# The last chunk ahead of a feed-forward: turned on TensorE, or by VectorE and DMAs through memory

## The chip, the cores and the metric

One Trainium2 chip, one of its cores. The metric is the device time of the whole program in microseconds (us), the median of several runs.

## The reference

Two transformer layers in float32 on 2048 tokens of width 448. Each layer is an attention with 16 query heads of width 28 that share one key and one value head, and a gated feed-forward of inner width 1792, both behind a layer normalization and added to the residual.

```python
x = A_x
x = x + _A_ref(_layernorm(x, axis=-1), A_wq, A_wk, A_wv, A_wo)
x = x + _B_ref(_layernorm(x, axis=-1), B_w_gate, B_w_up, B_w_down)
x = x + _A_ref(_layernorm(x, axis=-1), A_wq, A_wk, A_wv, A_wo)
x = x + _B_ref(_layernorm(x, axis=-1), B_w_gate, B_w_up, B_w_down)

def _B_ref(x, w_gate, w_up, w_down):
    g = _silu(x @ w_gate)
    u = x @ w_up
    return (g * u) @ w_down
```

## The kernel before

The 2048 tokens are cut into four chunks of 512 (`c` = 0 to 3), each of four tiles of 128 tokens. The residual `xres` stays in SBUF with tokens on the partitions. The matrix products want the normalized input turned, with the 448 features on the partitions, in three groups of 128 and one of 64, and split into a rounded high part and a rest (`xh`, `xl`), so that three products of rounded numbers stand for one of full ones. The last group of 64 features is kept twice, in the two halves of the partitions; `xd` holds a copy that this needs.

So between a normalization and a product a chunk has to be turned. The kernel has two ways for that:

- `flip` (L270) turns on TensorE: 16 transposes against an identity (L275) into PSUM banks, which ScalarE and VectorE then split into `xh` and `xl` (`flipped`, L278).
- `norm_steps(c, away=True)` (L213) turns without TensorE. For each of the four tiles VectorE normalizes into a side tile (`apply`, L234) and turns that in blocks of 32 x 32 into the tile `xn` (`turn`, L239). `send` (L248) writes `xn` to memory with four DMAs in an order that completes the turn, and `load` (L255, by way of `rows3`, L126) reads it back into another `xn` with two DMAs: one for the three full groups (L128), one that writes the last group to both halves (L129). `cut` (L265) splits from there.

Before the change chunks 0, 1 and 2 ahead of a feed-forward go the second way, spread over the attention's steps; the output projection of chunk 3 comes last, and chunk 3 goes the first way. Chunk 0 ahead of layer 1's attention goes the second way too (`hand_over`, L820). The side tile of the second way is `sg`, of which there is one, and which the feed-forward units use for their gate.

The feed-forward runs in units (`unit`, L853): one chunk of tokens by one slice of 128 of the inner width; two slices make a group, and a group goes over all four chunks. A unit with `xd` does on TensorE: first half of the gate and up products, then in the middle the first half of the down product of the unit before it (`pend`), then the second half of gate and up. Then ScalarE takes the gate's sigmoid product (L887), VectorE multiplies by up (L888), ScalarE rounds the product (L889), VectorE takes the rest (L892), and the second half of the earlier down product follows. Between the halves of a product ScalarE reads one column of each bank (`between`, L328), so that the second half does not begin before. After a chunk's last slice the sums are added to `xres` (L794 on VectorE, L797 and L798 on ScalarE and POOL).

The program's order on each engine and each DMA queue is the order in which this Python code issues instructions. Work that is to come later is put into lists: `soon` holds pairs of a number and a function, the number falls by one at the end of each unit, and the function is called there when it falls below zero; so 0 means the end of the next unit and 1 the end of the one after it. `mid[gi, c, n]` holds two functions for the middle of one unit, one ahead of the earlier unit's down product and one behind it.

`rest` (L918) begins the part of the feed-forward in which the change sits: the first units there are chunk 1 with slices 0 and 1, chunk 2 with slices 0 and 1, then chunk 3. Chunk 3 of the normalized input is prepared by these lines:

```python
            third, self.norms[3] = norm_steps(3)
            for f in third[:5]:
                f()
            self.soon.append([1, lambda: [f() for f in third[5:]]])
            self.mid[0, 2, 1] = [lambda ks=ks: self.turned(3, ks) for ks in ((0, 1), (2, 3))]
```

The statistics come at once, the normalization at the end of the unit of chunk 1 with slice 1, the transposes in the middle of the unit of chunk 2 with slice 1, two feature groups ahead of the down product and two behind it.

The DMAs named here are all issued from SyncE's queue, in order. The weight slices (`weights`, L157) are loaded there too, five DMAs each, into tiles of which there is one (`wr`, `wdr`); POOL splits them (L139, L140).

Of the kernel before, what the change touches and what calls it, by code (L numbers as in the profile page):

```python
# [8 lines left out]
F32 = mybir.dt.float32  # L9
# [6 lines left out]
P = 128  # L16
S = 2048
D = 448
# [34 lines left out]
def forward(  # L53
# [24 lines left out]
    pers = ctx.enter_context(tc.tile_pool(name="pers", bufs=1))  # L78
# [29 lines left out]
    def bank(cands, hold=False):  # L108

        for _ in cands:  # L110
            turn[cands] = (turn.get(cands, -1) + 1) % len(cands)
            b = cands[turn[cands]]
            if b not in live:
                if hold:
                    live.add(b)
                return b, banks[b]
        raise AssertionError("no bank")
# [5 lines left out]
    def dma(dst, src):  # L123
        nc.sync.dma_start(dst.bitcast(F32), src.bitcast(F32))

    def rows3(dst, src):  # L126
        n = src.shape[1]
        nc.sync.dma_start(dst[:, 0:3], src[0:384, :].rearrange("(k p) n -> p k n", p=P))  # L128
        nc.sync.dma_start(dst[:, 3], src[384:448, :][None].to_broadcast([2, 64, n]))  # L129

    def in_turn(cols):

        return cols.rearrange("p (n t) -> p t n", t=4)
# [71 lines left out]
    def xtile(pool, again=None):  # L205

        return (
            pool.tile([P, 4, 512], F32R, name="xh"),
            pool.tile([P, 3, 512], F32R, name="xl"),
            again,  # L210
        )

    def norm_steps(c, away=False):  # L213


        got = {}
        cs = slice(4 * c, 4 * c + 4)

        def stat(t):
            nc.vector.bn_stats(stats[:, 4 * c + t, :], xres[:, 4 * c + t, :])  # L220
            nc.vector.bn_aggr(mv[:, 4 * c + t, :], stats[:, 4 * c + t, :])

        def scale():
            rstd = pers.tile([P, 4], F32, name="rstd", bufs=2)
            nc.gpsimd.tensor_scalar(rstd, mv[:, cs, 1], 1.0, EPS, ALU.mult, ALU.add)
            nc.gpsimd.tensor_tensor(rstd, rstd, halfn, ALU.pow)
            got["r"] = rstd

        def apply(t):
            if t == 0:  # L230
                got["x"] = pers.tile([P, 4, 512], F32, name="xn")
            got["o"] = (pers.tile([P, 512], F32, name="sg") if away else got["x"][:, t, :])[:, 0:D]
            i, r = xres[:, 4 * c + t, :], got["r"][:, t : t + 1]
            nc.vector.tensor_scalar(got["o"], i, mv[:, 4 * c + t, 0:1], r, ALU.subtract, ALU.mult)  # L234
            if not away:
                nc.gpsimd.tensor_copy(got["x"][:, t, D:512], got["o"][:, 384:D])

        def turn(t):
            nc.vector.transpose(side()[:, :, :, t], got["o"].rearrange("p (k s) -> p k s", s=32))  # L239

        def side():
            return got["x"].rearrange("p t n -> p (t n)")[:, 0 : 4 * D].rearrange("p (k s t) -> p k s t", s=32, t=4)

        def send():
            turns.append(dram.tile([D, 512], F32, name=f"xt{len(turns)}"))
            got["xt"] = turns[-1]
            for a in range(4):
                nc.sync.dma_start(  # L248
                    got["xt"].rearrange("(k r) n -> r k n", r=32)[:, :, P * a : P * a + P],
                    side()[32 * a : 32 * a + 32].rearrange("p k s t -> p k (s t)"),  # L250
                )

        def load():
            got["raw"] = pers.tile([P, 4, 512], F32, name="xn")
            rows3(got["raw"], got["xt"])  # L255

        got["load"] = load
        fs = [lambda t=t: stat(t) for t in range(4)] + [scale]
        for t in range(4):
            fs += [lambda t=t: apply(t)] + [lambda t=t: turn(t)] * away  # L260
        return fs + [send] * away, got
# [3 lines left out]
    def cut(got, tiles, ks=range(4), copy=nc.scalar.copy):  # L265

        for k in ks:
            flipped(tiles, k, got["raw"][:, k, :], copy)

    def flip(got, tiles, ks=range(4)):  # L270

        for k in ks:
            pt = bank(wide[-1])[1]
            for t in range(4):
                nc.tensor.transpose(in_turn(pt)[:, t, :], got["x"][:, t, P * k : P * k + P], ident)  # L275
            flipped(tiles, k, pt, nc.scalar.copy)

    def flipped(tiles, k, pt, copy, steps=(0, 1)):  # L278

        xh, xl, xd = tiles  # L280
        twice = xd if k == 3 else None
        if 0 in steps and twice is None:
            copy(xh[:, k, :], pt)
        elif 0 in steps:
            copy(xh[0:64, k, :], pt[0:64, :])
            copy(xd[64:128, :], pt[64:128, :])
        if 1 in steps and k < 3:
            nc.vector.tensor_tensor(xl[:, k, :], pt, xh[:, k, :], ALU.subtract)
        elif 1 in steps:
            high = xh[64:128, k, :] if twice is None else xd[64:128, :]  # L290
            nc.vector.tensor_tensor(xh[64:128, k, :], pt[64:128, :], high, ALU.subtract)
# [40 lines left out]
    class Attention:  # L332
# [170 lines left out]
        def turned(self, c):  # L503
            if c in self.norms:
                flip(self.norms.pop(c), self.X[c])
# [245 lines left out]
    class FeedForward:  # L751
# [68 lines left out]
        def hand_over(self, c):  # L820

            a = self.nxt
            fs, got = norm_steps(c, c == 0)
            for f in fs[:5]:
                f()
            a.pool = self.stage
            a.X[c] = xtile(xpool if c < 2 else self.xbp)

            def ready():
                for f in fs[5:]:  # L830
                    f()
                a.norms[c] = got

            if c == 0:
                self.soon.append([1, lambda: [f() for f in fs[5:]]])
                self.soon.append([2, got["load"]])
                self.soon.append([4, lambda: cut(got, a.X[c])])
                self.soon.append([5, lambda: [a.project() for _ in range(3)]])
            elif c == 1:
                self.soon.append([2, ready])  # L840
            else:
                a.plan[4 * c - 4, 0] = [ready]

        def turned(self, c, ks=range(4)):
            flip(self.norms[c], self.X[c], ks)

        def flush(self):

# [68 lines left out]

        def rest(self, xb):  # L918
            self.stage = xb.enter_context(tc.tile_pool(name=f"stage{self.layer}", bufs=2, reuse_waits="tile"))
            self.xbp = xb.enter_context(tc.tile_pool(name=f"xb{self.layer + 1}", bufs=2, reuse_waits="tile"))  # L920
            xd = xb.enter_context(tc.tile_pool(name=f"xd{self.layer}", bufs=1, reuse_waits="tile"))
            self.xd = [xd.tile([P, 512], F32R, name=f"xd{c}") for c in range(NC)]
            for c in (0, 1):
                dma(self.xd[c][64:128, :], self.X[c][0][0:64, 3, :])
                self.X[c] = (*self.X[c][:2], self.xd[c])
            for c in (2, 3):
                self.X[c] = xtile(self.xbp, self.xd[c])
            cut(self.norms[2], self.X[2])
            third, self.norms[3] = norm_steps(3)
            for f in third[:5]:  # L930
                f()
            self.soon.append([1, lambda: [f() for f in third[5:]]])
            self.mid[0, 2, 1] = [lambda ks=ks: self.turned(3, ks) for ks in ((0, 1), (2, 3))]
            for gi, fs in enumerate(groups):
                if self.layer == 1 and fine is not None and gi in (2, 3):
                    self.verdict(gi == 3)
                    if gi == 3:
                        tc.mark_branch_hint_location("again", engines=(ET.Activation, ET.DVE, ET.Pool, ET.SP, ET.PE))
                for c in range(NC):
                    for n in range(len(fs)):  # L940
                        if gi or c:
                            self.unit(gi, c, n)
                if gi == len(groups) - 2 and self.nxt:
                    self.nxt.w = load_wqkv(xb.enter_context(tc.tile_pool(name="wqkv1", bufs=1, reuse_waits="tile")), None)[1]
            if self.nxt:
                self.nxt.project()
            self.flush()
# [7 lines left out]
    xb = ExitStack()  # L955
# [3 lines left out]
    fs, got = norm_steps(0)  # L959
# [28 lines left out]
    for c in range(1, NC):  # L988
        fs, got = norm_steps(c)
# [3 lines left out]
    for layer in range(2):  # L993
# [4 lines left out]
        xb = ExitStack()  # L998
# [30 lines left out]
```

## Time and profile before

| | us |
|---|---|
| median of 3 runs | 1986.77 |
| lowest and highest run | 1986.52, 1987.32 |
| span of the profiled execution, first to last instruction | 1984.8 |
| TensorE matmuls, busy | 1969.2 |
| ScalarE, busy | 1278.6 |
| VectorE, busy | 812.1 |
| POOL, busy | 528.7 |

The profiled execution's own time is its span; the timed runs lie some 2 us above it. In the rows of a timeline the columns are start and duration in us, engine, line, operation, the tiles it writes and reads, their shapes and how many such instructions are merged into the row; in brackets stands how long the engine was idle before it and what ended that. PE is TensorE, PEld its weight loads, DVE VectorE, ACT ScalarE, POOL GpSimd, and SPq the queue of SyncE, whose rows are the issues of DMAs and not their transfers. In the table by stretches of time, the columns are the stretch, its length, the busy time of PE, PEld, DVE, ACT and POOL with the number of instructions, the granted TensorE clock, the mean busy share of the 16 DMA engines, and GB/s.

### The profile page before, as it was taken

What the parts mean: (1) busy time and instruction counts of PE and PEld (TensorE: products, weight loads), DVE (VectorE), ACT (ScalarE), POOL (GpSimd) and SP (SyncE); (2) the same over time, 40 slices, a digit from 0 to 9 for tenths busy, and PEclk for the clock granted to TensorE, in tenths of its full rate; (3) what the DMA queues carried; (4) which work ended last, traced back from release to release, by engine and by line L of the source; (5) the groups of instructions that cost most, each with busy time, mean ns of one, the idle gap of its engine ahead of it and who ended that gap; (6) DMA issues with size and microseconds to landing.
All of it is one profiled execution on the core that took longest, in us unless ns stands there. A gap on an engine that the chain in (4) does not pass through costs nothing. (4 is left out here: it accounts for less than half of the span.)

```text
span 1984.8 us, 44687 instructions
## 1 busy us (share of the span) xinstructions
PE 1969.2 (99%) x18519; PEld 1322.9 (67%) x18519; DVE 812.1 (41%) x1410; ACT 1278.6 (64%) x2140; POOL 528.7 (27%) x571
## 2 busy tenths in 40 slices
PE   9999999999999999999999999999999999999998
PEld 7544545445458999999984444454454789988887
DVE  7444543544434222322554335445454432222222
ACT  4899797997953333333349998979979433333332
POOL 4212111132213233333341221111231232233320
PEclk9999999999999999999999999999999999999999
DMA  5101020121210011100131111102111101011102
GB/s 163 55 23 31 23 51 21 32 58 28 72 33 9 24 32 32 32 24 19 51 107 35 30 31 30 44 12 61 32 55 45 31 17 30 18 31 32 32 1 76
DMA packets 93382, 77.52 MB, mean 39 GB/s; under 512 B 23510, under 2 KB 76374, under 8 KB 93174
## 3 DMA queue, kind: packets, MB, share of 16 engines
q1 hardware_dynamic: 92886, 74.16, 13.5%
q8 instruction: 146, 2.39, 0.5%
q14 instruction: 62, 0.51, 0.1%
q10 hardware_dynamic: 288, 0.46, 0.1%
HBM read 55.06 MB, written 18.74 MB: 37 GB/s over the span
## 5 line engine op out<-in xcount | busy, mean ns | idle before, releaser
L647 PE MATMUL bank<-pt,vsb 128*32 128x512 f32 x4096 | 493.3, 598 | 0.5
L604 PE MATMUL bank<-qstack,keys 32*128 32x512 f32 x1536 | 484.2, 424 | 1.7 <-DVE xres L591 1.7
L604 PE MATMUL three<-qstack,keys 32*128 32x512 f32 x4608 | 461.4, 425 | 1.5 <-DVE vt L538 1.2
L604 PEld LDWEIGHTS three<-qstack,keys 32*128 32x128 f32 x4608 | 254.2, 182 | 295.0 <-ACT pt L617 181.1
L321 PE MATMUL bank<-xh,wgh 64*128 64x512 f32 x1728 | 437.5, 389 | 0.1
L611 ACT ACTIVATE pt<-three 128x1536 f32<-128x1536 f32 x256 | 372.2, 1454 | 0.6 <-ACT pt L617 0.3
L617 ACT ACTIVATE pt<-three 128x1536 f32<-128x1536 f32 x256 | 372.0, 1453 | 0.0
L321 PE MATMUL bank<-xh,wgl 64*128 64x512 f32 x1404 | 363.0, 390 | 0.0
L321 PE MATMUL bank<-wdh,h 64*128 64x448 f32 x1792 | 330.2, 364 | 1.4 <-ACT h L889 1.0
L321 PE MATMUL bank<-xl,wgh 64*128 64x512 f32 x1296 | 328.3, 389 | 0.0
L888 DVE TENSOR_TENSOR sg<-bank,sg 128x512 f32<-128x512 f32 x112 | 77.4, 691 | 497.6 <-ACT sg L887 488.4
L647 PEld LDWEIGHTS bank<-pt,vsb 128*32 128x32 f32 x4096 | 107.1, 109 | 250.2 <-issue 152.6
L613 DVE COPY raw<-bank 128x512 f32<-128x512 f32 x256 | 177.2, 692 | 230.7 <-PE bank L604 228.5
L321 PEld LDWEIGHTS bank<-xh,wgh 64*128 64x128 f32 x1728 | 256.9, 184 | 16.7 <-issue 0.9
L798 POOL TENSOR_TENSOR xres<-stage,xres 128x448 f32<-128x448 f32 x108 | 127.7, 1203 | 499.6 <-ACT stage L797 499.6
L657 DVE TENSOR_TENSOR o<-bank,o 128x512 f32<-128x512 f32 x224 | 154.9, 691 | 241.7 <-PE bank L647 237.1
L321 PEld LDWEIGHTS bank<-wdh,h 64*128 64x128 f32 x1792 | 240.5, 184 | 15.6 <-issue 2.0
L604 PEld LDWEIGHTS bank<-qstack,keys 32*128 32x128 f32 x1536 | 243.8, 183 | 4.6 <-DVE xres L591 3.6
L328 ACT COPY seen<-bank 128x1 f32<-128x1 f32 x664 | 81.0, 163 | 238.9 <-PE bank L321 236.4
L321 PEld LDWEIGHTS bank<-xh,wgl 64*128 64x128 f32 x1404 | 212.1, 184 | 13.8
L321 PE MATMUL bank<-wdl,h 64*128 64x448 f32 x896 | 215.6, 367 | 0.0
L887 ACT ACTIVATE sg<-bank 128x512 f32<-128x512 f32 x112 | 67.3, 601 | 223.2 <-PE bank L321 214.2
(127 smaller groups left out, 2259.3 us busy)
## 6 DMA issues: line engine op xcount, KB each, us to landing
o<-rd SPq DMA_DIRECT2D x32, 256.0 KB
qraw<-qd SPq DMA_DIRECT2D x128, 56.0 KB
qd<-stage SPq DMA_DIRECT2D x30, 224.0 KB
xt<-xn SPq DMA_DIRECT2D x28, 224.0 KB
wdr<-in_B_w_down_dram SPq DMA_DIRECT2D x28, 224.0 KB
xn<-xt SPq DMA_DIRECT2D x7, 768.0 KB
wr<-in_B_w_gate_dram SPq DMA_DIRECT2D x28, 192.0 KB
wr<-in_B_w_up_dram SPq DMA_DIRECT2D x28, 192.0 KB
```

What stands on the lines that cost most here:

```text
L321: nc.tensor.matmul(po, a, b, start=start, stop=stop, skip_group_check=True)
L328: nc.scalar.copy(seen[:, i : i + 1], po[:, 0:1])
L604: nc.tensor.matmul(three[:, j, :] if j < 3 else one, k[js, kp, ks], q[js, part, :], start=(z == 0), stop=(z == 2), tile_position=(32 * j, 0),)
L611: nc.scalar.activation(pt, three, AF.Exp, scale=SCALE)
L613: nc.vector.tensor_copy(raw, one)
L617: nc.scalar.activation(pt, three, AF.Exp, scale=SCALE)
L647: nc.tensor.matmul(po[32 * j : 32 * j + 32, :], vsb[:, n % NT, :], pts[n][j], start=(n == 2 * d), stop=(n > 2 * d), skip_group_check=True,)
L657: nc.vector.tensor_tensor(acc, in_turn(po), acc, ALU.add)
L798: nc.gpsimd.tensor_tensor(r, s, r, ALU.add)
L887: nc.scalar.activation(by_tile(sg), in_turn(pg[0]), AF.Silu)
L888: nc.vector.tensor_tensor(by_tile(sg), in_turn(pg[1]), by_tile(sg), ALU.mult)
```

## The change

In both layers chunk 3 ahead of the feed-forward goes the second way. Its normalization and block turns and the four sends are issued one unit sooner, at the end of the unit of chunk 1 with slice 0; the load at the end of the next unit; the splitting stands in the middle of the same unit as before. The side tile for this, and for chunk 0 ahead of layer 1's attention, is taken from a pool of its own with two buffers (`room`, 128 x 448 each) in place of `sg`. The 32 transposes of both layers and eight small copies on POOL (L236) go. The method `turned` of the feed-forward, which nothing calls any more, goes too.

```diff
-    def norm_steps(c, away=False):
+    def norm_steps(c, away=False, room=None):
...
-            got["o"] = (pers.tile([P, 512], F32, name="sg") if away else got["x"][:, t, :])[:, 0:D]
+            if room is not None:
+                got["o"] = room.tile([P, D], F32, name="side")
+            else:
+                got["o"] = (pers.tile([P, 512], F32, name="sg") if away else got["x"][:, t, :])[:, 0:D]
...
         def hand_over(self, c):
             a = self.nxt
-            fs, got = norm_steps(c, c == 0)
+            fs, got = norm_steps(c, c == 0, self.room if c == 0 else None)
...
-        def turned(self, c, ks=range(4)):
-            flip(self.norms[c], self.X[c], ks)
...
         def rest(self, xb):
             self.stage = xb.enter_context(tc.tile_pool(name=f"stage{self.layer}", bufs=2, reuse_waits="tile"))
+            self.room = xb.enter_context(tc.tile_pool(name=f"room{self.layer}", bufs=2, reuse_waits="tile"))
...
-            third, self.norms[3] = norm_steps(3)
+            third, got = norm_steps(3, True, self.room)
             for f in third[:5]:
                 f()
-            self.soon.append([1, lambda: [f() for f in third[5:]]])
-            self.mid[0, 2, 1] = [lambda ks=ks: self.turned(3, ks) for ks in ((0, 1), (2, 3))]
+            self.soon.append([0, lambda: [f() for f in third[5:]]])
+            self.soon.append([1, got["load"]])
+            self.mid[0, 2, 1] = [lambda ks=ks: cut(got, self.X[3], ks) for ks in ((0, 1), (2, 3))]
```

## The prediction

> **What bounds the kernel now.** I read the page first: busy shares, then the chain of work that ended last.
>
> ```profile
> PE 1969.2 (99%) x18519; PEld 1322.9 (67%) x18519; DVE 812.1 (41%) x1410; ACT 1278.6 (64%) x2140; POOL 528.7 (27%) x571
> PE 48%; ACT 0%; DVE 0%; issue 0%; POOL 0%; DVEq 0%; ACTq 0%
> ```
>
> TensorE works through the whole span, and what the chain can name is nearly all its own. So an edit is worth what it takes off TensorE's sequence, less every new wait of that sequence. Averages say no more than this; the change sits in a stretch of some 30 us at the start of each feed-forward, so I went to the timeline there. I call the units that follow the attention output A, B, C, D, E: chunk 1 slices 0 and 1, chunk 2 slices 0 and 1, chunk 3 slice 0. The transposes stand in the middle of D, and E is the first unit that needs chunk 3. In the middle of every unit TensorE starts the down product of the unit before it (`bank<-wdh,h`); these are my marks.
>
> ```profile
> 605.03 0.38 PE L321 MATMUL bank<-wdh,h 64*128 64x448 f32 x2
> ...
> 612.33 0.38 PE L321 MATMUL bank<-wdh,h 64*128 64x448 f32 x2
> ...
> 612.74 0.58 PE L321 MATMUL bank<-wdh,h 64*128 64x448 f32 x4
> ...
> 619.72 1.09 PE L275 MATMUL bank<-ident,xn 128*128 128x128 f32 x8
> ...
> 622.17 1.09 PE L275 MATMUL bank<-ident,xn 128*128 128x128 f32 x8
> ...
> 627.18 0.18 PEld L321 LDWEIGHTS bank<-xh,wgh 64*128 64x128 f32 x1 [0.37 <-DVE sg L888]
> ...
> 629.60 0.36 PE L321 MATMUL bank<-wdh,h 64*128 64x448 f32 x1
> ```
>
> The mark comes at 605.03 in B and 612.33 in C: a unit takes 7.30 us. Two units on, E's mark would be at 626.93; it is at 629.60. **The transposes cost TensorE 2.67 us a layer**: two blocks of eight, 1.09 us each as shown, their seams, and 0.37 us in E, whose bank VectorE had not yet read (four extra bank picks inside D turn the rotation back onto D's own pair).
>
> **What goes.** 32 transposes in the two layers: 2 x 2.67 = 5.34 us off the sequence. With them go POOL's eight copies and ScalarE's reads of PSUM; both engines have idle time here, so nothing for those.
>
> **What is added before B's product.** Normalization and block turns of chunk 3, four pairs, now stand on VectorE at the end of A, ahead of B's gating product (L888). Such pairs run already at the hand-over to layer 1:
>
> ```profile
> 964.57 0.52 DVE L234 TENSOR_SCALAR sg<-xres,mv,rstd 128x448 f32<-128x448 f32 x1
> ...
> 969.84 0.98 DVE L239 STREAM_TRANSPOSE xn<-sg 128x448 f32<-128x448 f32 x1
> 970.85 3.06 SPq L248 DMA_DIRECT2D xt<-xn  x4
> 970.91 0.60 ACT L887 ACTIVATE sg<-bank 128x512 f32<-128x512 f32 x1 [3.83 <-DVE xn L239]
> 971.54 0.69 DVE L888 TENSOR_TENSOR sg<-bank,sg 128x512 f32<-128x512 f32 x1 [0.72 <-ACT sg L887]
> ...
> 972.27 0.62 ACT L889 CAST h<-sg 128x512 fp32r<-128x512 f32 x1 [0.76 <-DVE sg L888]
> ...
> 972.92 0.69 DVE L892 TENSOR_TENSOR h<-sg,h 128x512 fp32r<-128x512 f32 x1 [0.15 <-ACT h L889]
> ...
> 972.94 0.90 PE L321 MATMUL bank<-wdh,h 64*128 64x448 f32 x2 [0.18 <-ACT h L889]
> ...
> 973.68 0.99 PE L321 MATMUL bank<-wdh,h 64*128 64x448 f32 x4
> ...
> 977.24 0.38 SPq L128 DMA_DIRECT2D xn<-xt  x1
> ```
>
> Four pairs last from 964.57 to 970.82: 6.25 us. Where they would start in A, and the steps of B that wait behind them:
>
> ```profile
> 604.11 0.62 DVE L794 TENSOR_TENSOR xres<-bank,xres 128x448 f32<-128x448 f32 x1
> 609.42 0.69 DVE L888 TENSOR_TENSOR sg<-bank,sg 128x512 f32<-128x512 f32 x1 [4.69 <-ACT sg L887]
> ...
> 610.14 0.62 ACT L889 CAST h<-sg 128x512 fp32r<-128x512 f32 x1 [0.76 <-DVE sg L888]
> ...
> 610.80 0.69 DVE L892 TENSOR_TENSOR h<-sg,h 128x512 fp32r<-128x512 f32 x1 [0.69 <-ACT h L889]
> ```
>
> They start at 604.75, end at 611.00, and L888 moves from 609.42 to 611.02. L892 follows 1.38 us behind, at 612.40, and TensorE takes the residual 0.76 us after that starts (972.92 to 973.68): 613.16, wanted at 612.74. A stall of 0.42 us, unless something later is worse.
>
> **What is added before E.** Chunk 3 now reaches E by memory. SyncE sends at 611.03. At the hand-over it took 6.39 us from the first send (970.85) until the load was issued (977.24), because the load waits until all four sends have landed: here the load goes out at 617.42. When does it land? The load has two parts, the second (64 rows, written to two places) on few DMA engines. The same load at the hand-over, where nothing else moved, in the table by stretches (the last two columns are the DMA share and GB/s):
>
> ```profile
> 979.20:981.20 2.00, 2.00 (x22) 1.77 (x19) 0.69 (x1) 0.22 (x1) 0.00 (x0) 1.00 0.92 345
> ...
> 982.20:986.20 4.00, 4.00 (x38) 3.63 (x37) 0.84 (x2) 1.00 (x5) 0.00 (x0) 1.00 0.13 49
> 986.20:987.20 1.00, 1.00 (x12) 0.87 (x10) 0.84 (x2) 1.00 (x3) 0.00 (x0) 1.00 0.04 16
> ```
>
> After two busy microseconds the share is 0.13, two engines of sixteen, until 986.5 or so; with the landing I take 987.0, 9.8 us after the issue. Nobody sees this tail at the hand-over, where the data is used a unit and more later. So the earliest landing L here is 617.42 + 9.8 = 627.2.
>
> And here SyncE is not idle behind the load. The five transfers of the next weight slice, which went out before the units began, are now queued behind it; they are issued from 618.4.
>
> ```profile
> 395.77 0.47 SPq L128 DMA_DIRECT2D xn<-xt  x1
> ...
> 406.00:408.00 2.00, 2.00 (x27) 0.70 (x19) 0.69 (x1) 2.00 (x4) 0.00 (x0) 1.00 0.15 53
> 408.00:409.00 1.00, 1.00 (x16) 0.59 (x17) 0.00 (x0) 1.00 (x2) 0.00 (x0) 1.00 0.11 41
> ...
> 554.18 0.60 SPq L679 DMA_DIRECT2D o<-rd  x1
> 559.33 1.29 POOL L686 TENSOR_TENSOR o<-o 128x512 f32<-128x512 f32 x1 [24.68 <-DVE o L657]
> ...
> 581.80 0.59 SPq L679 DMA_DIRECT2D o<-rd  x1
> ...
> 583.64 0.59 SPq L128 DMA_DIRECT2D wr<-in_B_w_gate_dram  x1
> ...
> 588.67 1.29 POOL L686 TENSOR_TENSOR o<-o 128x512 f32<-128x512 f32 x1 [25.99 <-DMA o<-rd]
> ...
> 638.38 1.05 POOL L139 TENSOR_SCALAR wgh<-wr 128x1024 fp32r<-128x1024 f32 x1
> ```
>
> A copy like ours (`o<-rd`) was used 5.15 us after its issue at 554.18 with nothing behind it, and 6.87 us after 581.80 with these same weight loads behind it: at least 1.7 us, or a third, more. And the load of 395.77, with other transfers around it, ran until 409, some 13.5 us. So L lies between 627.2 (quiet) and 617.4 + 13.5 = 630.9; a third on 9.8 gives 630.5, 1.7 us on it 628.9. I take 629.5, nearest to the weight-load rows. The weights themselves are wanted by POOL at 638.38, which leaves over 5 us.
>
> [...]
>
> What waits for L? ScalarE, in order: it stops in D at the last quarter of chunk 3, and D's own gating (L887 to L892) is queued behind. The last steps, from SBUF, where layer 0's chunk 2 is prepared this way:
>
> ```profile
> 597.41 0.62 ACT L286 CAST xd<-xn 64x512 fp32r<-64x512 f32 x1
> ...
> 598.06 0.69 DVE L291 TENSOR_TENSOR xh<-xn,xd 64x512 fp32r<-64x512 f32 x1 [0.30 <-ACT xd L286]
> ```
>
> From L: 0.05 to notice (an estimate), two casts of half tiles at 0.62 each, L291 0.03 + 0.69, so chunk 3 is complete at L + 2.01, and TensorE stands in E before that. D's gating: L888 at L + 2.04, L889 0.72 later, L892 at L + 3.42. TensorE can take the first half 0.67 us after L889 starts (972.27 to 972.94), at L + 3.43, and the residual at L + 4.18, where it wants it 0.41 us (612.33 to 612.74) behind the first. E's mark is thus at about **L + 3.77**. Before it was 629.60: break-even is L = 625.8. The earlier stall of 0.42 us is swallowed in this one. With L = 629.5 the mark comes at 633.27, **3.67 us later than before in each layer**, the transposes' gain already taken off. Layer 1 has the same stretch:
>
> ```profile
> 1601.15 1.09 PE L275 MATMUL bank<-ident,xn 128*128 128x128 f32 x8
> ...
> 1611.03 0.36 PE L321 MATMUL bank<-wdh,h 64*128 64x448 f32 x1
> ```
>
> Both rows stand 981.43 us behind their twins of layer 0. Twice 3.67 = 7.3 us.
>
> **The hand-over with its own buffers.** There the gate (L887) waited for the turns, since both used `sg`. With other buffers it runs early, and L888 follows the last turn: 970.84 in place of 971.54. TensorE stalled on what hangs on L888, so 0.7 us come back, once.
>
> **Sum.** 7.3 - 0.7 = +6.6 us. The profiled execution's span is 1984.8 us; the median of the runs, 1986.77, lies 2.0 us above it, which I leave as it is: 1986.8 + 6.6 = 1993.4 us. What a measurement here can tell from no change is about 0.2%, 4.0 us.
>
> **Rivals.**
>
> 1. Hidden, and so not slower. If the memory path lands by L = 625.8, nothing is lost; by about 622 only the 0.42 us remain, and the time is 1986.8 - 5.34 + 0.84 - 0.7 = 1981.6. For it: nobody waits for this load anywhere now. Against: even the quiet load of 977.24 would be 1.4 us late. 6%.
> 2. Quiet tail. The weights do not disturb it, L = 627.2: 2 x (630.97 - 629.60) - 0.7 = +2.0 us, 1988.8. For it: two engines at 0.13 do not crowd anybody. Against: the row of 581.80. 21%.
> 3. The stall slows TensorE's clock. In my forecast TensorE halts in E near 627.7 and goes on at L + 2.1 = 631.6, almost 4 us, where the rows above show no halt over 0.4. The granted clock is at its best in all 40 slices of the page, so the trace does not show what such a halt does. Half the clock for as long as the halt would lose about 2 us a layer: 1997.4, or 2000 with L = 630.9.
>
> ```profile
> PEclk9999999999999999999999999999999999999999
> ```
>
> [...] 17%.
>
> My forecast, a load slowed by the weights and a clock that holds, has 53%; 3% are left for what I do not see.
>
> **How the numbers follow.** The likeliest case gives 1993.4, its own range by L from 628.5 to 630.9 is 1991 to 1996. The range reaches down to rival 2 and up to rival 3 with the later landing: 1988.5 to 2000.0. Slower by over 0.2% needs L above 628.2: the forecast, rival 3 and part of what is unseen, 0.73. Within 0.2%: rival 2, 0.21. Faster: rival 1, 0.06.
>
> **What would show it.** No L275 rows after the projections; L888 of B at about 611.0; the load issued at 617.4, with the weight loads right behind it; ScalarE's L285 in D waiting for a DMA until near 629.5; in E a wait of TensorE for VectorE's L291 of 3 to 4 us and a shorter one for L889; E's mark near 633.3 in layer 0. At the hand-over L888 directly behind the last turn. I am wrong if L285 does not wait, or if E's mark comes before 629.6.

## The result and the profile after

The changed kernel takes 1991.58 us (median of 6 runs, 1990.94 to 1995.30), the kernel before 1986.61 us on the same chip (6 runs, 1986.46 to 1987.32): a ratio of 1.003, 95% interval 1.002 to 1.004, so 5.0 us slower. The profiled execution has a span of 1989.1 us, 4.3 us more than before's 1984.8. The changed kernel stands three lines lower in its file: before's L234, L239, L248, L285, L286, L291 and L321 are L237, L242, L251, L288, L289, L294 and L324, and L887 to L892 are where they were.

First the busy shares and the chain of work that ended last, from the page of the changed kernel:

```profile
PE 1969.1 (99%) x18487; PEld 1266.7 (64%) x18487; DVE 818.6 (41%) x1418; ACT 1273.2 (64%) x2140; POOL 524.9 (26%) x563
PE 47%; DMA 1%; DVE 1%; ACT 0%; issue 0%; SPq 0%; POOL 0%; DVEq 0%; ACTq 0%
```

TensorE has 32 instructions fewer, and yet its busy time is the same to 0.1 us: what it does must have become slower somewhere. And the chain, which ran through no DMA before, now has 1% of them. The timeline of the first units of layer 0 shows which (VectorE, SyncE, ScalarE and TensorE one after the other; time origins of two traces differ, here B's mark stands at 604.60 where before had 605.03, so 0.43 us is added to compare with the prediction):

```profile
604.22 0.82 DVE L237 TENSOR_SCALAR side<-xres,mv,rstd 128x448 f32<-128x448 f32 x1
...
607.22 0.43 DVE L237 TENSOR_SCALAR side<-xres,mv,rstd 128x448 f32<-128x448 f32 x1
...
608.99 0.99 DVE L242 STREAM_TRANSPOSE xn<-side 128x448 f32<-128x448 f32 x1
609.83 0.68 DVE L888 TENSOR_TENSOR sg<-bank,sg 128x512 f32<-128x512 f32 x1
```

```profile
610.01 3.12 SPq L251 DMA_DIRECT2D xt<-xn  x4
616.38 0.38 SPq L128 DMA_DIRECT2D xn<-xt  x1
616.80 0.59 SPq L129 DMA_DIRECT2D xn<-xt  x1
617.43 0.46 SPq L128 DMA_DIRECT2D wr<-in_B_w_gate_dram  x1
...
619.42 3.97 SPq L128 DMA_DIRECT2D wr<-in_B_w_up_dram  x1
```

```profile
621.03 1.14 ACT L286 CAST xh<-xn 128x512 fp32r<-128x512 f32 x2 [1.34 <-DMA xn<-xt]
...
626.46 0.62 ACT L288 CAST xh<-xn 64x512 fp32r<-64x512 f32 x1 [3.52 <-DMA xn<-xt]
...
629.20 0.62 ACT L889 CAST h<-sg 128x512 fp32r<-128x512 f32 x1 [0.86 <-DVE sg L888]
```

```profile
611.90 0.38 PE L324 MATMUL bank<-wdh,h 64*128 64x448 f32 x2
...
627.13 0.49 PE L324 MATMUL bank<-xh,wgh 64*128 64x512 f32 x1 [0.94 <-ACT xh L288]
628.49 0.49 PE L324 MATMUL bank<-xh,wgh 64*128 64x512 f32 x1 [0.87 <-DVE xh L294]
...
629.87 0.47 PE L324 MATMUL bank<-wdh,h 64*128 64x448 f32 x2 [0.64 <-ACT seen L331]
```

The reader is to see four things. The turns take 5.76 us (604.22 to 609.98), C's mark at 611.90 is a plain 7.30 us behind B's, and so B's product costs TensorE nothing. The load goes out at 616.38 and ScalarE stands 3.52 us for its second part, until 626.46: 10.1 us after the issue. TensorE stands in E three times, 2.45 us in all. And E's mark comes at 629.87, that is 630.30 in before's time, 0.70 us later than its 629.60.

A mark that comes 0.70 us late in each layer doesn't explain 4 us. The table by stretches does, cut at the edges at which the trace shows the granted clock to change (columns: stretch; its length; busy us of PE, PEld, DVE, ACT and POOL with counts; granted clock; DMA share; GB/s):

```profile
627.16:630.57 3.41, 1.87 (x8) 0.74 (x8) 2.07 (x3) 1.89 (x5) 0.00 (x0) 1.00 0.36 99
630.57:633.98 3.41, 3.39 (x18) 2.81 (x20) 0.00 (x0) 0.45 (x4) 0.00 (x0) 0.50 0.02 6
633.98:637.39 3.41, 3.41 (x34) 2.92 (x32) 1.19 (x2) 1.06 (x2) 0.00 (x0) 1.00 0.00 0
```

After the three waits TensorE runs at half its clock for one stretch of 3.41 us: 18 matmuls where the next stretch has 34. The 16 that are missing are some 1.6 us of the full rate. In before the granted clock falls only behind the last matmul, which begins at 1977.93: it is 1.00 from 1978.5 to 1981.5 and 0.55 on average from there to the end, 1984.8. Measured from the start of A's gate (L887) to that of E's, which follows E's mark by some 4 us, the whole costs layer 0 2.45 us (before's two rows first, then those of the changed kernel):

```profile
601.49 0.60 ACT L887 ACTIVATE sg<-bank 128x512 f32<-128x512 f32 x1 [1.96 <-PE bank L321]
633.55 0.60 ACT L887 ACTIVATE sg<-bank 128x512 f32<-128x512 f32 x1 [1.96 <-PE bank L321]
```

```profile
601.06 0.60 ACT L887 ACTIVATE sg<-bank 128x512 f32<-128x512 f32 x1 [1.96 <-PE bank L324]
635.57 0.60 ACT L887 ACTIVATE sg<-bank 128x512 f32<-128x512 f32 x1 [2.73 <-PE bank L324]
```

Before 32.06 us, after 34.51. In the same way for every kernel of this study, against the first profile of before (positive is lost time). Each column is a stretch between two starts of L887, which lie in before at 601.49 and 633.55 (A to E), at 961.75 and 992.45 (hand-over), at 992.45 and 1582.93 (layer 1's attention) and at 1597.52 and 1622.29 (C to the unit behind E); from A to C, 1582.93 to 1597.52, no kernel differs:

| kernel | layer 0, A to E | hand-over | layer 1's attention | layer 1, C to behind E | half-clock stretches of 3.41 us, layers 0 and 1 |
|---|---|---|---|---|---|
| before, second profile | 0.00 | -0.03 | +0.49 | +0.02 | 0, 0 |
| after | +2.45 | -1.08 | +1.07 | +2.03 | 1, 1 |
| path_only | +3.17 | 0.00 | +0.54 | +2.20 | 2, 1 |
| room_only | -0.01 | -1.09 | +0.68 | -0.02 | 0, 0 |
| held | +2.09 | -1.08 | +1.61 | +3.35 | 1, 2 |
| filler | +0.75 | -1.08 | +1.37 | +0.98 | 0, 0 |
| filler4 | +0.76 | -1.09 | +0.31 | +2.33 | 0, 1 |
| rotate | -0.45 | -0.02 | +0.58 | -0.46 | 0, 0 |
| spread | -2.15 | -1.10 | +0.98 | -2.49 | 0, 0 |
| best | -2.89 | -1.08 | +1.44 | -2.89 | 0, 0 |

The column of the attention is the one that no edit orders; more on it below, in the part on the prediction.

### The profile page after: what moved, and what is told of

Its sections match the earlier page's. It is cut to its first block, busy times and chain, and to the rows that moved or that the text cites. A ratio compares the mean times of both kernels' runs of the same rounds, so it can differ in the third digit from the quotient of the medians.

```text
span 1989.1 us, 44636 instructions
## 1 busy us (share of the span) xinstructions
PE 1969.1 (99%) x18487; PEld 1266.7 (64%) x18487; DVE 818.6 (41%) x1418; ACT 1273.2 (64%) x2140; POOL 524.9 (26%) x563
## 5 line engine op out<-in xcount | busy, mean ns | idle before, releaser
L324 PE MATMUL bank<-xh,wgh 64*128 64x512 f32 x1728 | 342.7, 390 | 3.7 <-ACT xh L288 1.8
L324 PE MATMUL bank<-xh,wgl 64*128 64x512 f32 x1404 | 299.6, 391 | 0.0
L324 PE MATMUL bank<-wdh,h 64*128 64x448 f32 x1792 | 296.0, 365 | 2.5 <-ACT seen L331 1.5
L888 DVE TENSOR_TENSOR sg<-bank,sg 128x512 f32<-128x512 f32 x112 | 77.4, 691 | 488.2 <-ACT sg L887 479.0
L324 PE MATMUL bank<-xl,wgh 64*128 64x512 f32 x1296 | 256.6, 390 | 0.0
L331 ACT COPY seen<-bank 128x1 f32<-128x1 f32 x664 | 75.8, 164 | 246.5 <-PE bank L324 245.3
L887 ACT ACTIVATE sg<-bank 128x512 f32<-128x512 f32 x112 | 67.2, 600 | 214.3 <-PE bank L324 209.1
L689 POOL TENSOR_TENSOR o<-o 128x512 f32<-128x512 f32 x32 | 41.2, 1287 | 581.3 <-DMA o<-rd 525.3
L619 ACT ACTIVATE pt<-bank 128x512 f32<-128x512 f32 x256 | 151.0, 590 | 64.5 <-PE bank L607 64.4
L324 PEld LDWEIGHTS bank<-xh,wgh 64*128 64x128 f32 x1728 | 165.3, 185 | 35.9 <-ACT xh L288 2.6
L324 PEld LDWEIGHTS bank<-wdh,h 64*128 64x128 f32 x1792 | 171.4, 185 | 25.0 <-ACT seen L331 3.1
```

The costliest lines, as they stand in the source:

```text
L324: nc.tensor.matmul(po, a, b, start=start, stop=stop, skip_group_check=True)
L331: nc.scalar.copy(seen[:, i : i + 1], po[:, 0:1])
L619: nc.scalar.activation(pt1, one, AF.Exp, scale=SCALE)
L887: nc.scalar.activation(by_tile(sg), in_turn(pg[0]), AF.Silu)
L888: nc.vector.tensor_tensor(by_tile(sg), in_turn(pg[1]), by_tile(sg), ALU.mult)
```

## The experiments

My theory after the result: the tail of the load is all that goes wrong, from 621.5 to 624 at a DMA share of 0.13, on average two engines of sixteen. It stops ScalarE (3.52 us), then TensorE (2.45 us), and the halts halve the clock (0.50 for 3.41 us). The rival: VectorE's turns, the sends or the memory path as such.

**spread: the tail taken away.** The 64 rows that go to two places are read by two DMAs of 64 partitions.

```diff
-            rows3(got["raw"], got["xt"])
+            nc.sync.dma_start(got["raw"][:, 0:3], got["xt"][0:384, :].rearrange("(k p) n -> p k n", p=P))
+            for half in (slice(0, 64), slice(64, P)):
+                nc.sync.dma_start(got["raw"][half, 3], got["xt"][384:448, :])
```

> The changed kernel, with the second part of the load (64 rows to two places) as two DMAs of 64 partitions each instead of one with a leading dimension of two. Theory 1 (two engines carry a 5 us tail, TensorE waits for it and its clock falls to half for one window of 3.4 us): the whole load lands some 5 us after its issue instead of 10, ScalarE waits for it about 1.3 us in unit D, TensorE not at all, no stretch at half clock; per layer 2.7 us less than the kernel before, the hand-over 1.1 us less, so 1980 to 1982 us. Theory 2 (the turns on VectorE and the way through memory cost by themselves, whatever the tail): 1990 to 1992 us, near the changed kernel.

Measured 1983.02 us (11 runs, 1981.37 to 1984.59) against 1986.49, ratio 0.9984 (0.9975 to 0.9993): from slower to faster, by this alone. ScalarE's timeline in D and the mark of E:

```profile
621.29 1.14 ACT L288 CAST xh<-xn 128x512 fp32r<-128x512 f32 x2 [1.93 <-DMA xn<-xt]
...
623.07 0.63 ACT L290 CAST xh<-xn 64x512 fp32r<-64x512 f32 x1
```

```profile
626.52 0.44 PE L326 MATMUL bank<-wdh,h 64*128 64x448 f32 x2
```

The half tiles (here L290, L291) are cast at 623.07 without any wait. The time is 1 us above what I expected. What is left is the 1.93 us wait on the load's first part: E's mark is at 626.52, 22.25 us behind B's (604.27), where three units are 21.88, and by the table the layers gain 2.15 and 2.49 us where the last experiment, without this wait, gains 2.89. The theory stands: as one DMA the second part ended in a tail at a DMA share of 0.12 to 0.16 (next experiment), as two it has landed by the time ScalarE is through with the first part. Why the one DMA ran at so low a share, the runs do not show.

**held: is the tail long because of the weights behind it?** The forecast had it so. Here the five weight transfers are kept back by a copy that reads chunk 3's finished tile.

```diff
             if c == NC - 1 and fc + FG + 1 < NF:
+                if gi == 0 and n == 0:
+                    hold = dram.tile([1, 4], F32, name=f"hold{self.layer}")
+                    self.pend.append(lambda: nc.sync.dma_start(hold, self.xd[3][64:65, 0:4].bitcast(F32)))
                 self.pend.append(lambda: self.W.__setitem__(fc + FG + 1, weights(fc + FG + 1)))
```

> The changed kernel with the five weight transfers that stood behind chunk 3's load held back: a copy of four numbers out of chunk 3's finished tile goes ahead of them on SyncE, so that none of them is issued before the load has landed and ScalarE's last cast is done. It settles the step on which the forecast rested, that weights queued behind slow the load. Theory (they don't: the load's second part is 128 packets on two engines, and these take 10 us with or without company): ScalarE's last casts in D begin 10 us after the issue as before, near 626.4, E's mark stays at 629.9 in the trace's own time, and the waits of TensorE in E are the same three. Rival (the weights share the two engines and cost a third or so, and it is the quiet load that is shorter than I read it): the casts begin near 624, E's mark comes near 627.5, TensorE hardly waits and the time is 1983 to 1985.

One run, 1992.83 us. SyncE's queue, ScalarE, and the table by stretches:

```profile
616.75 0.38 SPq L128 DMA_DIRECT2D xn<-xt  x1
...
627.94 0.23 SPq L909 DMA_DIRECT2D hold<-xd  x1
628.22 0.40 SPq L128 DMA_DIRECT2D wr<-in_B_w_gate_dram  x1
```

```profile
626.66 0.62 ACT L288 CAST xh<-xn 64x512 fp32r<-64x512 f32 x1 [3.44 <-DMA xn<-xt]
```

```profile
621.20:623.20 2.00, 2.00 (x21) 1.73 (x19) 1.23 (x2) 1.88 (x7) 0.00 (x0) 1.00 0.13 50
623.20:625.20 2.00, 2.00 (x22) 1.88 (x20) 0.74 (x2) 0.02 (x1) 0.00 (x0) 1.00 0.16 57
625.20:626.20 1.00, 1.00 (x12) 0.89 (x10) 0.00 (x0) 0.00 (x0) 0.00 (x0) 1.00 0.12 45
```

With nothing behind it the load takes 9.9 us from issue to cast (616.75 to 626.66), and 10.1 in layer 1 (1600.89 to 1610.99); with five transfers behind it, in the changed kernel, 10.1 in both layers. They cost it 0.2 us at most, not a third. TensorE's three waits in E are there again, 0.67, 0.86 and 0.64 us. From 621.2 to 626.2, the last 5 us, the DMA share is 0.12 to 0.16, on average two engines of sixteen or a little more. The rival is out.

**path_only and room_only: the two halves of the change.** path_only is the changed kernel with chunk 0 at the hand-over back on `sg`; room_only is the kernel before with the side tiles at the hand-over alone.

```diff
-            fs, got = norm_steps(c, c == 0, self.room if c == 0 else None)
+            fs, got = norm_steps(c, c == 0)
```

> The changed kernel, with the hand-over's chunk 0 back on the side tile sg (the two own buffers serve chunk 3 alone). Theory 1: the 1.1 us that the hand-over gained are lost again, 1992.7 us. Theory 2 (the gain at the hand-over is given back in layer 1, where the changed kernel lost 1.0 us against the one before): 1991.6 us, no difference.

```diff
-            fs, got = norm_steps(c, c == 0)
+            fs, got = norm_steps(c, c == 0, self.room if c == 0 else None)
```

> The kernel before, with the two own buffers at the hand-over alone; chunk 3 is turned on TensorE as before. Theory 1: 1.1 us faster than before, 1985.5 us. Theory 2 (given back in layer 1): 1986.6 us. My prediction's term was 0.7: 1985.9 us.

path_only took 1992.97 us (1992.04 to 1993.86), ratio 1.0032 (1.0020 to 1.0044); room_only 1985.76 (1984.86 to 1986.88), ratio 0.9996 (0.9987 to 1.0006), which the time alone does not tell from nothing. Nor is path_only's time a clean measure, since in its profile layer 0 lost one more stretch at half clock than the changed kernel's. The traces tell. In path_only the hand-over has before's picture, in room_only the gate (here L890) no longer waits for a turn:

```profile
973.96 0.60 ACT L887 ACTIVATE sg<-bank 128x512 f32<-128x512 f32 x1 [3.83 <-DVE xn L242]
...
975.98 0.90 PE L324 MATMUL bank<-wdh,h 64*128 64x448 f32 x2 [0.18 <-ACT h L889]
```

```profile
968.50 0.60 ACT L890 ACTIVATE sg<-bank 128x512 f32<-128x512 f32 x1 [1.96 <-PE bank L324]
```

The table above says how much: 1.08 to 1.10 us in all kernels with the side tiles, nothing in those without.

**filler: work laid into the wait.** E's first half repeats one pair of matmuls twelve times, which adds products to the bank.

```diff
+                if (gi, c, n) == (0, 3, 0):
+                    for l in (lists[0], lists[3]):
+                        l[9:9] = [l[8]] * 12
```

> The changed kernel; in the first unit of chunk 3 of each layer TensorE repeats one pair of small products (a rest times the input) twelve times, 2.7 us of work laid into the place where it waits for the load, so the sums of that unit contain those terms thirteen times. Theory 1a (the waits cost 0.7 us a layer beyond the transposes, the half clock that follows them 1.7 us): no stretch at half clock, 1988.2 us. Theory 1b (the half clock does not come from the waits, or the waits alone are the cost): 1991.6 us or up to 5 us more.

1988.34 us (1986.78 to 1989.87), ratio 1.0009 (0.9999 to 1.0018), as expected: 2.7 us of additional TensorE work in each layer made the kernel 3 us faster than the changed one. The one wait left and the clock behind it:

```profile
631.16 0.47 PE L324 MATMUL bank<-wdh,h 64*128 64x448 f32 x2 [0.35 <-ACT seen L331]
```

```profile
628.00:632.00 4.00, 3.61 (x32) 2.54 (x30) 2.07 (x3) 2.33 (x6) 0.00 (x0) 1.00 0.34 90
632.00:636.00 4.00, 4.00 (x38) 3.44 (x40) 0.05 (x1) 1.05 (x5) 0.00 (x0) 1.00 0.01 3
```

So of layer 0's 2.45 us the late load itself, less the transposes that went, is 0.75 and the halved clock 1.70; of layer 1's 2.03 they are 0.98 and 1.05.

**filler4: how much of a wait halves the clock?** The same with four repeats.

```diff
-                        l[9:9] = [l[8]] * 12
+                        l[9:9] = [l[8]] * 4
```

> The changed kernel with four instead of twelve repeated pairs in E (which adds products to a bank, so its output is not the reference's): 0.9 us of TensorE work lie in the first of E's three waits. The first wait (0.94) should go, the others (0.87 and 0.64) stay, 1.5 us of waiting in place of 2.45. [...]

One run, 1988.74 us. Both layers keep the same two waits, 0.87 and 0.64 us; the first two rows are layer 0, the last two layer 1:

```profile
628.51 0.50 PE L324 MATMUL bank<-xh,wgh 64*128 64x512 f32 x1 [0.87 <-DVE xh L294]
...
629.89 0.47 PE L324 MATMUL bank<-wdh,h 64*128 64x448 f32 x2 [0.64 <-ACT seen L331]
...
1610.09 0.50 PE L324 MATMUL bank<-xh,wgh 64*128 64x512 f32 x1 [0.87 <-DVE xh L294]
...
1611.46 0.47 PE L324 MATMUL bank<-wdh,h 64*128 64x448 f32 x2 [0.64 <-ACT seen L331]
```

Yet layer 0 keeps the full clock and layer 1 loses it for 3.41 us, from 1611.88. The table, first in layer 0, then in layer 1, in steps of 2 us around the waits, and last the 3.41 us ahead of the fall and those at half clock:

```profile
626.00:628.00 2.00, 1.64 (x13) 0.94 (x9) 0.23 (x1) 1.47 (x3) 0.00 (x0) 1.00 0.16 44
628.00:630.00 2.00, 0.84 (x5) 0.41 (x7) 1.28 (x3) 1.10 (x4) 0.00 (x0) 1.00 0.43 140
630.00:632.00 2.00, 1.95 (x18) 1.42 (x19) 0.56 (x1) 0.37 (x4) 0.00 (x0) 1.00 0.07 22
632.00:634.00 2.00, 2.00 (x20) 1.66 (x18) 0.00 (x0) 0.08 (x2) 0.00 (x0) 1.00 0.00 0
...
1608.00:1610.00 2.00, 1.17 (x8) 0.41 (x5) 0.65 (x1) 1.83 (x3) 0.00 (x0) 1.00 0.22 62
1610.00:1612.00 2.00, 1.26 (x7) 0.59 (x7) 1.29 (x3) 0.74 (x3) 0.00 (x0) 0.97 0.39 119
1612.00:1614.00 2.00, 2.00 (x12) 1.65 (x12) 0.14 (x1) 0.16 (x1) 0.00 (x0) 0.50 0.04 13
...
1608.47:1611.88 3.41, 1.85 (x10) 0.77 (x8) 1.82 (x3) 2.16 (x6) 0.00 (x0) 1.00 0.33 98
1611.88:1615.30 3.42, 3.42 (x20) 2.67 (x18) 0.26 (x1) 0.45 (x4) 0.00 (x0) 0.50 0.03 12
```

TensorE is busy 2.48 us of the 4 us around the waits in layer 0 and 2.43 us of 4 in layer 1, and only layer 1 falls to 0.50, behind 3.41 us of which TensorE was busy 1.85. The changed kernel's first fall came behind 1.87 us of 3.41. So, as far as this one pair of layers shows, neither the longest wait (0.87 us in both) nor the sum of the waits (1.51 us in both) tells whether the clock falls. What does was not shown.

**rotate: the 0.37 us of the banks.** The kernel before, with E's bank pair no longer that of D.

```diff
             flip(self.norms[c], self.X[c], ks)
+            if 3 in ks:
+                turn[LOW] = (turn[LOW] + 2) % 4
```

> The kernel before, with the rotation of the four banks set on by two after the transposes of D, so that E takes the other pair. It separates the 0.37 us that the prediction booked as part of the transposes' 2.67 us. Theory: the wait of 0.37 us for VectorE's gating product at E's start is gone and E's mark comes at 629.2 (629.60 before), so that the transposes themselves cost 2.3 us a layer; 1986 in all. Rival: the wait is only the last of several that end together, another takes its place and E's mark stays at 629.6.

One run, 1986.64 us, which by itself shows no gain. B's and E's mark:

```profile
605.61 0.38 PE L321 MATMUL bank<-wdh,h 64*128 64x448 f32 x2
...
629.94 0.37 PE L321 MATMUL bank<-wdh,h 64*128 64x448 f32 x2
```

The distance is 24.33 us where before has 24.57, and at E's gate, some 4 us later, 0.45 us are gone, in both layers. Of the 2.67 us that I booked for the transposes, 0.24 at the mark were the bank rotation's (I had put this at 0.37, and at 629.2 for the mark: in before's time, 0.58 us earlier than this trace's, it is 629.36), and one line gets them without any new path; another 0.2 us, which I had not booked, went behind the mark, where before's row is of one matmul (629.60) and rotate's of two (629.94). That this costs the 0.2 us is argued, not shown.

**before_again: the attention's drift.**

> The kernel before, unchanged, profiled a second time. In every run so far the stretch of layer 1's attention came out 0.6 to 1.4 us longer than in the first profile of the kernel before. Theory (two executions differ by that much): this second profile shows that stretch longer by about 1 us too, with a span of 1985 to 1986. Rival (what changed at the hand-over costs 1 us later): the second profile repeats the first within 0.3 us there.

One run, 1986.21 us, span 1984.5. The stretch of layer 1's attention was 0.49 us longer than in the first profile with not a line changed: half of what I took for an effect.

**best: the load cut by feature group as well.** The three groups of 128 rows come by a DMA each, so ScalarE can begin with the first.

```diff
-            nc.sync.dma_start(got["raw"][:, 0:3], got["xt"][0:384, :].rearrange("(k p) n -> p k n", p=P))
+            for k in range(3):
+                nc.sync.dma_start(got["raw"][:, k], got["xt"][P * k : P * k + P, :])
```

> The kernel of spread with the load's first part cut by feature group, three transfers of 128 partitions in place of one, so that ScalarE can begin on the first group before the whole load has landed. Theory: ScalarE's wait in D (1.93 us in spread) shrinks to under 0.3, D's gating is on time, E's mark comes 0.4 us earlier than the 626.5 of spread: 1982.2. [...]

1981.72 us (10 runs, 1980.04 to 1984.31) against 1986.27, ratio 0.9977 (0.9967 to 0.9987): 4.5 us faster than before, and 10 us faster than the changed kernel. SyncE, ScalarE and E's mark:

```profile
616.49 1.29 SPq L259 DMA_DIRECT2D xn<-xt  x3
617.83 1.11 SPq L261 DMA_DIRECT2D xn<-xt  x2
```

```profile
619.79 1.15 ACT L289 CAST xh<-xn 128x512 fp32r<-128x512 f32 x2
```

```profile
626.68 0.38 PE L327 MATMUL bank<-wdh,h 64*128 64x448 f32 x2
```

The cast on ScalarE has no wait in brackets any more, and E's mark is 21.88 us behind B's (604.80): three units of 7.29, nothing between. Each layer gives 2.89 us. This is the change with its cost taken off. That best beats spread is read from the traces; the intervals of the two times overlap.

## Why the prediction was right or wrong

Right were the direction and the place: slower by 0.3%, by way of ScalarE waiting in D for the load's last part and TensorE in E for ScalarE. But the direction too owes much to the clock, which the forecast took to hold: filler, where it holds, is not told from before (1.0009, 0.9999 to 1.0018). The chain behind L held to 0.03 us: with L at 626.41 (0.05 us ahead of the cast, the prediction's estimate, which no run measures) L889 was due at L + 2.76 = 629.17 (629.20 measured) and the first half of E's down product at L + 3.43 = 629.84 (629.87).

Wrong was the step "the weights queued behind slow the load by a third". It put 12.1 us between issue and landing; without the weights behind it the load took 9.9 and 10.1 us in the two layers (held), with them 10.1 in both. What failed in it is the comparison: the copy that took 6.87 us instead of 5.15 was another copy, elsewhere, and its delay need not have come from the weights: SyncE had issued two other copies (`xd<-xh`, at 582.43) between it and them. What delayed it was not tested. The quiet tail at the hand-over, the same load with the same tail, was the nearer row, and I had it. Rival 2 was right there, with at most 0.2 us for five transfers behind. Together with an issue 0.6 us sooner (616.81 in before's time for 617.42), since the turns took 5.76 us and not 6.25, L is 626.84 in before's time where I took 629.5. So E's mark moved by +0.70 us, not by +3.67, and E's gate, where the clock holds (filler), by +0.75.

Wrong the other way was to let the clock hold: rival 3, which I gave 17% and tied to a halt of almost 4 us, came about with 1.5 us of waits (0.87 and 0.64) in the 3.41 us ahead of layer 0's fall, of which TensorE was busy 1.87. The rival's half clock for as long as the halt, which gives the range its upper end, was an estimate that no run shows; the changed kernel's granted clock is 0.50 for 3.41 us in each layer. Against filler the half clock made up 1.70 us in layer 0 and 1.05 in layer 1. So two errors offset each other in part, -2.9 and +1.7 us in layer 0, -2.7 and +1.05 in layer 1. That the range held the time was in good part luck, for it had another make-up than the forecast: rival 2 and rival 3 at once, a case that I had not priced.

B's stall of 0.42 us: none; L888 came at 609.83, 610.26 in before's time, and not at 611.02. Two side tiles instead of one let VectorE begin the next normalization while a turn runs, L237 fell from 0.52 to 0.43 us (at 607.22 it begins ahead of the end of the turn of 606.39, which lasts 0.99), and the pitch of a pair from 1.57 to 1.30.

The hand-over: 0.7 us forecast, 1.08 measured. The mechanism was right (the gate runs early, and L888 comes directly behind the last turn), and the shorter pairs, which I had not counted, bring the rest: L888 now also follows the gate by 0.03 us, and the unit takes a plain 7.29 us (L887 at 963.77 and 971.06), so nothing is lost there any more.

```profile
971.06 0.60 ACT L887 ACTIVATE sg<-bank 128x512 f32<-128x512 f32 x1 [1.96 <-PE bank L324]
971.69 0.69 DVE L888 TENSOR_TENSOR sg<-bank,sg 128x512 f32<-128x512 f32 x1
```

By the table the profiled execution adds up to 2.45 - 1.08 + 1.07 + 2.03 = 4.5 us of the 4.3; the prediction had 3.67 - 0.7 + 3.67. The 1.07 us of the attention were in no forecast. Profiles without the new path show 0.00 to 0.68 there, those with it 0.31 to 1.61, in no order that follows an edit; whether part of it belongs to the change stays open.

## What to carry to other kernels

Ask of every transfer that comes onto the path at what DMA share it runs, to its end: the copy of 64 rows to two places, whose last 4 to 5 us ran at about 0.13, is harmless as long as nobody waits for it (the hand-over), and here held ScalarE for 3.52 us when somebody did; two copies of 64 partitions did the same work without that wait. Price a new wait of TensorE at its length, and look at the granted clock around its end: with the changed kernel's waits of 2.45 and 2.36 us it was 0.50 for 3.41 us, which cost 1.70 and 1.05 us on top. Two errors of opposite sign can look like a good forecast, so compare the terms, not only the sum.

## What the runs showed of the hardware

- From the last of E's waits on the changed kernel's granted clock is 0.50 for 3.41 us in each layer, from 630.57 (0.70 us behind that wait's end) and from 1613.61 (0.06 us ahead of it). In the 3.41 us ahead TensorE was busy 1.87 us in layer 0 and 1.23 in layer 1; ahead of the falls of filler4 (layer 1) and path_only (layer 0) 1.85 and 1.61 us. The rows of the changed kernel's layer 1:

```profile
1610.20:1613.61 3.41, 1.23 (x4) 0.48 (x4) 1.38 (x2) 2.44 (x6) 0.00 (x0) 1.00 0.34 99
1613.61:1617.02 3.41, 3.35 (x18) 2.78 (x20) 0.69 (x1) 0.57 (x7) 0.00 (x0) 0.50 0.05 15
1617.02:1620.44 3.42, 3.42 (x34) 2.92 (x32) 0.77 (x2) 0.65 (x2) 0.00 (x0) 1.00 0.01 2
```

- Once halved, the clock did not always come back after 3.41 us: in path_only's layer 0 it is 0.50 from 629.03 to 635.86, 6.83 us, and held's layer 1 has two stretches of 3.41 us. In the first half of path_only's TensorE is busy 3.09 us and still has a wait of 0.33 us; the changed kernel's stretches, busy 3.39 and 3.35 us, were followed by the full clock.

```profile
629.03:632.45 3.42, 3.09 (x15) 2.01 (x15) 1.13 (x2) 0.90 (x4) 0.00 (x0) 0.50 0.19 65
632.45:635.86 3.41, 3.41 (x18) 2.72 (x18) 0.00 (x0) 0.28 (x3) 0.00 (x0) 0.50 0.00 0
```

- Like waits in the two layers of one execution did not cost alike: filler4 has 0 and 1 such stretches, held 1 and 2. This does not by itself explain how far the runs of one kernel lie apart: those of the changed kernel spread over 4.4 us, with the mean granted clock at 0.996 in the two longest and 0.997 in the rest, but those of best spread over 4.3 us at 0.999 and 1.0.
- One of SyncE's issues was long while the tail ran: the third weight DMA of the changed kernel took 3.97 us to issue (619.42), the same one in held, issued when the tail was over, 0.47, and in spread, without the tail, 1.01.
